# A third chunk's gelu by the activation table instead of the tanh formula, in a fused attention and gated feed-forward block

## The chip, the cores and the metric

One core of one Trainium2 chip. The metric is the device time of one execution in microseconds, the median of several runs. Lower is better.

## What is computed

A pre-norm block over 2048 tokens of width 640 in bf16: 32 heads of 20 for the attention, 1728 hidden columns for the gated feed-forward. There is no mask.

```python
def _A_ref(x, wqkv, wo):
    qkv = (x @ wqkv).reshape(B, S, 3, H, Dh).transpose(2, 0, 3, 1, 4)
    q, k, v = qkv[0], qkv[1], qkv[2]
    scores = jnp.einsum("bhqd,bhkd->bhqk", q, k) * (Dh ** -0.5)
    p = _softmax(scores, axis=-1)
    o = jnp.einsum("bhqk,bhkd->bhqd", p, v)
    return o.transpose(0, 2, 1, 3).reshape(B, S, D) @ wo
def _B_ref(x, w_gate, w_up, w_down):
    g = jnp.einsum("bsd,df->bsf", x, w_gate)
    u = jnp.einsum("bsd,df->bsf", x, w_up)
    return jnp.einsum("bsf,fd->bsd", jax.nn.gelu(g, approximate=True) * u, w_down)
x = A_x
h = x + _A_ref(_layernorm(x), A_wqkv, A_wo)
h2 = h + _B_ref(_layernorm(h), B_w_gate, B_w_up, B_w_down)
```

## The kernel before

The queries are cut into eight chunks (SIZES): 512, then five of 256, then two of 128 tokens. Counted from zero, chunks 0 to 7 start at tokens 0, 512, 768, 1024, 1280, 1536, 1792 and 1920. The third chunk of the title is chunk 2, tokens 768 to 1023. The heads come in eight groups of four. A slot is a chunk with as many groups as fill 512 columns, so there are 32 slots: eight for chunk 0, four for each chunk of 256, two for each of 128.

In a slot the scores of four heads are made in row groups of TensorE (L1081) in units of two or three PSUM banks. ScalarE takes the exponential of a unit of 1024 or 1536 columns (in the profile L450, `pts<-ps` and `rege<-ps`, which are two buffers). Part of the tiles go to VectorE instead (D_SLOT says how many), which makes an exponential from integer steps: one step out of PSUM (L992) and four terms (L450, TENSOR_SCALAR on 2048 columns); SUMS says how many pairs of terms are added first, and D_RING how many of these tiles take a bank of a ScalarE unit, which then shrinks from three tiles to two. The product with the values accumulates in bank 6 (L450, `ps<-pts,v_all` and the like). At a slot's end the sums are copied to `osb`, normalised and sent on; for the last slots of a chunk by transposes on TensorE (L1181), a reciprocal (L1187) and products (L1191).

When a chunk's attention is done, `post` makes the rest of the block for it, as background work beside the next chunk's attention: output projection (L758, L753 in its column form, L1274 in the last chunk), residual sum (L1285), layernorm, transposes, gate, gelu, up and down projection. The gate, up and down matmuls are L753 in the column form (four groups of 32 columns) and L1336, L1331 and L1405 otherwise; COL says from which chunk width on the column form is used and FULL which chunks do not use it. The gelu is made in one of two ways. Before TANH_FROM the gate is copied out of PSUM (L1379), and once all of it is out, the activation table's gelu runs over up to 2048 columns at a time. From TANH_FROM on, the gate is halved on the way out (L1373), and `gelu` makes three products and two scalar steps on VectorE and a tanh on ScalarE for pieces of up to 1024 columns. The up projection is multiplied in afterwards (L1390). The last chunk, which has no attention beside it, uses the gelu table (L1359, L1362), and its layernorm a root on ScalarE; its table loads are started early by one-column activations (`warmsq`, `warmge`).

The order on every engine is written out by a planner in the kernel (`Sched`). It goes through all operations with planned durations, priorities (P_...) and ages (QK_LEAD, PE_AGE, SD_AGE, SD_ROW: one value per slot), and emits for each engine one fixed queue with semaphore waits. An engine never passes a waiting instruction. The planner fills idle TensorE time with extra matmuls that change nothing. For ScalarE it knows modes, and a change of mode is planned with 1.28 us; a mode called "exp2", which only the formula's tanh has, is left out of that:

```python
op("act", I("activation", z, z, ACT.Tanh), c_act(w) + 0.04, -1, mode="exp2", reads=[zk], writes=[zk])
...
if o.mode is not None and o.mode != "exp2":
    if mode[e] not in (None, o.mode):
        o.dur += MODE_SWITCH[e]
    mode[e] = o.mode
```

The table loads themselves are put in when the program is compiled, wherever an activation needs another set than the one that is loaded.

At the start, maxima of the keys are taken (L792), combined (`kd`), and a bound for the scores is made from them (L891, L895); the first score waits for that. The first value projections (L907) are made beside it; `V_ACT` names those whose eviction ScalarE makes (L915) instead of VectorE (L917), `V_HOLD` from which set on they wait.

Of the kernel before, what the change touches and what calls it, by code (L numbers as in the profile page):

```python
# [18 lines left out]
DRAIN = {"pe": 0.165, "act": 0.118, "dve": 0.085, "pool": 0.05, "sp": 0.0}  # L19
WARM_WIN, WARM_MIN = 3.4, 0.5  # L20
PAD_WIN, PAD_MIN = 3.4, 0.42
QK_LEAD = (0.68, 0.72,) + (0.65,) * 4 + (0.72,) * 7 + (0.6,) * 4 + (0.72,) * 6 + (0.68, 0.68, 0.55, 0.55, 0.68, 0.65, 0.65, 0.68, 0.68,)
ACT_GAP = .012
PE_AGE = (2.5,) + (3.0,) * 5 + (5.0,) * 8 + (3.0,) * 3 + (5.0, 5.0, 2.0, 2.0,) + (5.0,) * 4 + (1.5, 1.5, 3.5, 3.0,) + (1.5,) * 3
SD_AGE = (0.6, 0.6, 0.3,) + (0.6,) * 6 + (0.8,) + (0.6,) * 5 + (1.0, 0.3, 0.6, 0.8, 0.6, 1.0, 0.5, 1.0, 1.0, 0.5,) + (0.6,) * 3 + (0.8,) * 4
SD_ROW = (0,) * 5 + (0.6,) * 4 + (1.5, 0.6, 0.6, 1.5,) + (0.6,) * 16 + (1.0, 0.6, 0,)
STOP = None


# [22 lines left out]
class Sched:  # L52
# [14 lines left out]
    def op(self, eng, fns, dur, prio, reads=(), writes=(), acq=(), rel=(), after=(), sem=None, lat=None, mode=None, util=0.0, rows=()):  # L67
        if eng == "dve" and rel and prio > self.ev:
            prio = self.ev
        o = Op()  # L70
        o.i = len(self.ops)
        o.eng, o.dur, o.lat, o.sem = eng, dur, DRAIN[eng] if lat is None else lat, sem
        o.util = util
        o.mode = mode
        o.rows = rows
        o.tag = writes[0] if writes else None
        o.fns = fns if isinstance(fns, list) else [fns]
        o.prio = (prio, o.i)
        deps = set(after)
        for r in reads:  # L80
            if r in self.lw:
                deps.add(self.lw[r])
        for w in writes:
            if w in self.lw:
                deps.add(self.lw[w])
            deps.update(self.rd.get(w, ()))
        for r in reads:
            self.rd.setdefault(r, []).append(o.i)
        for w in writes:
            self.lw[w] = o.i  # L90
            self.rd[w] = []
        deps.discard(o.i)
        o.deps = deps
        o.acq = list(acq)
        o.rel = list(rel)
        o.succ = []
        o.ready = 0.0
        self.ops.append(o)
        return o.i

    def schedule(self):
# [29 lines left out]
        while done < total:  # L131
# [6 lines left out]
            for e in ENGINES:  # L138
# [8 lines left out]
                while ready[e]:  # L147
# [18 lines left out]
                    if got and o.mode == "row" and 0 < p[0] < 1 and scores > 1 and t - o.ready < (  # L166
                            at(SD_AGE) if mode[e] != "row" else at(SD_ROW) if row_end[o.rows[0]] > max([row_start + 0.01] + [freed[b] for b in got]) + 0.02 else 0):
                        skipped.append((p, i))
# [89 lines left out]
                if e == "act":  # L258
                    act_end = max(act_end, t) + o.dur + ACT_GAP
                    o.fin = act_end + o.lat  # L260
                    due = act_end + (0.917 if o.dur > 1.2 else 1.344) - at(QK_LEAD) if o.mode == "exp" else None
                heapq.heappush(events, free[e])
# [104 lines left out]
PV_QUADS = 2  # L367
PR, PR2 = 13, 6
D_SLOT = (1,) + (3,) * 26 + (2, 3, 3, 0, 0,)
SUMS = (0,) + (1,) * 4 + (2, 2, 0, 0, 1, 0,) + (1,) * 3 + (0, 1, 1, 2, 3, 1, 0, 1, 1, 0, 2, 2, 1, 0, 1, 0, 3, 0,)  # L370
HOP = 3.2
D_LAT = 0.3
RECIP_MAGIC = float(0x7EF311C3)
# [6 lines left out]
RESV = 0.0  # L380
QK_LAT = 0.165
VN = 4
D_RING = (9,) * 4 + (6, 6,) + (9,) * 6 + (6,) * 16 + (12,) + (6,) * 3
D_FIRST = 0
D_SPAN = (16,) + (18,) * 13 + (17,) + (18,) * 4 + (19,) * 4 + (18,) * 7 + (17, 17,)
D0 = 8
P33 = ()
TANH_FROM = 768
GELU_A = 2.0 * 0.7978845608028654
GELU_B = 4.0 * GELU_A * 0.044715  # L390

P_EV = 1.8
P_QK, P_PV, P_TAIL, P_PRO, P_EPI, P_LN, P_BG = 0, 1, 1.2, 1.5, 2, 2.5, 3
P_KQ = (2, 3, 3, 3)
P_V1 = 3.0
P_V0 = 2.5
P_ON = 2.1
V_ACT = (0,)
XN_DVE = (7, 10, 13, 15)
VP = (0, 2, 5, 8)  # L400
V1 = ((0, 0, 0, 0, 0, 0, 0, 0, 1, 1, 1, 1, 1, 1, 1, 1), (2, 2, 2, 2, 3, 3, 3, 3, 3, 3, 3, 3, 4, 4, 4, 4))
X_LAT = 3.0
O_LAT = 3.2
HOP_L = 3.2
XP_PE = (6,)
HOLD = 3
P_KP = 1.6
K1_AFTER = 3
Q1_HOLD = 1
V_HOLD = 3  # L410
XD = ()
P_NOW = 1.05
P_K0 = 1.0
VB = (6, 7, 5)
K1_ACT = ()
FULL = (5,)
GROUPS = ((0, 4), (4, 7), (11, 5))
AG = (11, 5)
P_RS = 1.45
XORD = (0, 3, 1, 2)  # L420
P_DV = 0.5
P_ADD = 1.8
P_ST = 1.9
P_OUT = 2.5
LN_DVE = (0, 1, 2, 3, 4, 5, 6)
LATE = (0, 1, 2, 3, 4)

# [1 line left out]
def bass_sequential_preLN__mha_block__glu_gated_geglu__prompt_kernel(  # L429
# [12 lines left out]
    with ExitStack() as es:  # L442
# [492 lines left out]
        for s_, (c, gs) in enumerate(slots):  # L935
            mine = list(dict.fromkeys(x[1:3] for x in tiles if x[0] == s_))
            n = D_SLOT[s_]
            d_kb[s_] = [mine[(2 * i + 1) * len(mine) // (2 * n)] for i in range(n)]
            k = min(SUMS[s_], 2 * n)
            d_sums[s_] = [(i + 1) * k // max(n, 1) - i * k // max(n, 1) for i in range(n)]  # L940
# [5 lines left out]
        while rem:  # L946
# [8 lines left out]
            n = len(bs)  # L955
            ring.append(k[1] < want and n == 3 and (k[1] + 1) * D_RING[s_] // max(nd, 1) > k[1] * D_RING[s_] // max(nd, 1))
            n -= ring[-1]
# [170 lines left out]
        def spread(s, c, gs, nq):  # L1128
# [13 lines left out]
            for j in range(4):  # L1142
                h(bsum[32 * j:32 * j + 32, :], rdr[s, j].partition_broadcast(32), [("rdr", s)], ("bs", j), "sd", 0.36)
            op("dve", I("tensor_tensor", on16[:], osb[:, s, :], bsum[:], ALU.mult), c_dve(512), P_ON,
               reads=[("osb", s)] + [("bs", j) for j in range(4)], writes=["on16"])
# [4 lines left out]
        def epilogue(s_, bk):  # L1150
# [46 lines left out]
            if tail or not last:  # L1197
# [8 lines left out]
            op("sp", I("dma_start", oT[:, 0:na, tok], src[0:128 * na, :].rearrange("(a p) s -> p a s", p=128)), 0.4, P_EPI,  # L1206
               reads=ars, writes=hk, sem=f"oT{c}", lat=O_LAT + nq * 0.004, after=tuple(e_ops) if c == 0 else ())
            op("sp", I("dma_start", oT[0:pf, na, tok], src[128 * na:f0, :]), 0.4, P_EPI,
               reads=ars, writes=hk, sem=f"oT{c}", lat=O_LAT + nq * 0.004, after=tuple(e_ops) if c == 0 else ())
            todo = [(a, 0) for a in range(na + 1, NA)] + [(na, pf)]  # L1210
# [41 lines left out]
        def post(c, banks, tail):  # L1252
            p = P_TAIL if tail else P_LN
            q0, nq = CHUNKS[c]
            nt = nq // 128
            cl = nq >= COL and c not in FULL
            tb = base(c)
            hb = 1792 * tb
            first = tuple(e_ops) + tuple(last_qk[0]) + tuple(d_ops) if c == 0 else ()
            for tt in range(tb, tb + nt):  # L1260
# [5 lines left out]
                for hf in range(2):  # L1266
                    bk = Bank(*banks, after=LATE)
                    key = ("bk", sc_id())
                    if tail:
# [3 lines left out]
                        for a in range(NA):  # L1273
# [9 lines left out]
                    list(chain(bk, key, 320, [(oT[:, a, tt * 128:(tt + 1) * 128], wo[:, a, hf * 320:(hf + 1) * 320])  # L1283
                                              for a in range(NA)], [("hnT", tt), "wo"], p if tail else P_OUT, after=(sc.lw[("h", tt, hf)],), col=cl))
                    op("dve", lambda eng, bk=bk, tt=tt, hf=hf, i=i: eng.tensor_tensor(  # L1285
                        h_sb[:, tt, hf * 320:(hf + 1) * 320], bank(bk, 320), h_sb[:, tt, hf * 320:(hf + 1) * 320], ALU.add),
                       c_dve(320), p if tail else P_ADD, reads=[key, ("h", tt, hf)], writes=[("h", tt, hf)], rel=[bk], after=first)
                if tail:
# [76 lines left out]
            else:  # L1365

                cp, gl = [], []
                for k in range(nb):
                    bg, kg = mms(k, wg, "wg", tuple(x for key in hkeys(k) for x in sc.rd.get(key, ())))
                    w = cols(k)  # L1370
                    fv = hv(k, w)
                    if q0 >= TANH_FROM:
                        op("dve", lambda eng, bg=bg, fv=fv, w=w: eng.tensor_scalar(fv, bank(bg, w), 0.5, None, ALU.mult),  # L1373
                           c_dve(w), p, reads=[kg], writes=hkeys(k), rel=[bg])
                        if k % 2 or k == nb - 1:
# [4 lines left out]
                                 reads=[kg], writes=hkeys(k), rel=[bg], after=first))  # L1380
                for ks in [] if q0 >= TANH_FROM else [list(range(i, min(i + 4, nb))) for i in range(0, nb, 4)]:
                    w = 512 * (ks[-1] - ks[0]) + cols(ks[-1])
# [57 lines left out]
        for kts in v_sets(0):  # L1440
            proj_v(kts, 0, VB, P_EPI if kts[0] < VN else P_V0, "act" if kts[0] in V_ACT else "dve",
                   (sc.lw[HELD],) if HOLD and kts[0] >= V_HOLD else ())
        
        ui = 0
        for s_, (c, gs) in enumerate(slots):
# [37 lines left out]
            if gs[-1] == NG - 1:  # L1483
                tail = c == len(CHUNKS) - 1
                sc.ev = P_EV
                if c == 0:
# [36 lines left out]
```

## Time and profile before

| | |
|---|---|
| median of 3 runs | 866.83 us (866.38 to 867.52) |
| the profiled execution | 867.75 us, span 866.0 us |
| TensorE busy | 838.5 us (97%) |
| ScalarE busy | 838.4 us (97%), 8 table loads |
| VectorE busy | 750.4 us (87%) |
| granted TensorE clock | 0.998 |
| HBM traffic | 44 GB/s over the span |

In the rows of groups, `out<-in` are tiles by the program's names, then partitions x elements, the count, the busy time, the mean nanoseconds of one and the idle time of the engine ahead of it with its releaser. In the rows of the timeline, the first number is the start in microseconds, the second the length from the first start to the last end of a run of like instructions. The length of an instruction has a small overlap with the next one of its engine, so the distance from start to start is what it costs the queue. `regw`, `rege` and `qt_all` are large buffers that hold other things at other times: the gate of the feed-forward is in `rege`, the formula's intermediate in `qt_all`.

### The profile page before, as it was taken

The numbers are of one execution on the slowest core, as the hardware profiler recorded it, in microseconds if no ns is written. First come the engines' busy times: TensorE is split into PE (matmuls) and PEld (weight loads), VectorE is DVE, ScalarE is ACT, GpSimd is POOL, SyncE is SP. The second block draws the span as 40 slices with busy tenths as digits, with TensorE's granted clock in tenths as the row PEclk, the third lists the DMA queues.
The fourth block names the chain that finished last, engine by engine and source line by source line (L and its number), as shares of the span: only waits on it lengthen the run. The fifth ranks groups of instructions, "written<-read, shape, count | busy, mean of one in ns | idle before, by whom it ended". The sixth has DMA issues, their size and how long they took to land.

```text
span 866.0 us, 35545 instructions
## 1 busy us (share of the span) xinstructions
PE 838.5 (97%) x16215; PEld 420.4 (49%) x16215; DVE 750.4 (87%) x1372; ACT 838.4 (97%) x806; POOL 89.6 (10%) x268
## 2 busy tenths in 40 slices
PE   7999999999999899999999999999999999999998
PEld 5532332322343344445455555555554556666667
DVE  8769999999999799797899989999999897988344
ACT  7999999999999999999999999999999999999992
POOL 5001111110001110101002000011102110010000
PEclk9999999999999999999999999999999999999999
DMA  7212021223202642001110102010101101030000
GB/s 274 81 47 61 29 76 47 59 61 92 58 16 60 160 147 80 16 18 36 53 42 16 36 8 61 5 35 17 49 19 24 58 12 27 20 47 11 2 18 17
DMA packets 50173, 43.19 MB, mean 50 GB/s; under 512 B 21316, under 2 KB 44640, under 8 KB 50024
## 3 DMA queue, kind: packets, MB, share of 16 engines
q1 hardware_dynamic: 50024, 40.93, 16.8%
q8 instruction: 127, 2.08, 1.0%
q14 instruction: 22, 0.18, 0.1%
HBM read 27.95 MB, written 10.26 MB: 44 GB/s over the span
## 4 chain that ended last, share of the span: by engine, by line
ACT 51%; PE 39%; DVE 8%; issue 1%
ACT pts L450 35%; ACT rege L450 15%; PE ps L1081 11%; PE ps L450 10%; PE ps L753 9%; PE ps L758 3%; DVE qt_all L450 2%; DVE rege L450 2%; PE ps L907 1%; PE ps L1336 1%; DVE rege L992 1%; DVE qt_all L992 1%; PE ps L1405 1%; ACT qt_all L450 1%; PE ps L675 1%
## 5 line engine op out<-in xcount | busy, mean ns | idle before, releaser
L450 ACT ACTIVATE pts<-ps 128x1024 bf16<-128x1024 f32 (+1 forms) x496 | 558.5, 1240 | 2.8 <-PE ps L1081 2.2
L1081 PE MATMUL ps<-qt_all,kt_all 32*128 32x256 bf16 (+2 forms) x4096 | 304.0, 273 | 11.5 <-ACT pts L450 5.6
L450 ACT ACTIVATE rege<-ps 128x1024 bf16<-128x1024 f32 (+1 forms) x222 | 248.3, 1199 | 0.7 <-PE ps L1081 0.3
L1081 PEld LDWEIGHTS ps<-qt_all,kt_all 32*128 32x128 bf16 x4096 | 103.2, 92 | 202.8 <-ACT pts L450 90.6
L992 DVE TENSOR_SCALAR rege<-ps 128x512 int16<-128x512 f32 x220 | 148.5, 684 | 20.0 <-PE ps L1081 18.6
L450 PE MATMUL ps<-rege,v_all 128*21 128x256 bf16 (+2 forms) x2197 | 139.3, 286 | 0.5 <-DVE rege L450 0.5
L450 PE MATMUL ps<-pts,v_all 128*21 128x256 bf16 (+2 forms) x2403 | 124.8, 273 | 1.0 <-DVE osb L450 0.8
L753 PE MATMUL ps<-rege,regw 128*32 128x256 bf16 (+1 forms) x2600 | 120.5, 296 | 1.6 <-DVE rege L992 0.5
L992 DVE TENSOR_SCALAR qt_all<-ps 128x512 int16<-128x512 f32 x128 | 86.7, 683 | 11.0 <-PE ps L1081 10.2
L450 DVE TENSOR_SCALAR rege<-rege 128x2048 int16<-128x2048 int16 x141 | 94.5, 687 | 1.5 <-PE ps L450 0.8
L753 PEld LDWEIGHTS ps<-rege,regw 128*32 128x32 bf16 x2600 | 60.4, 96 | 34.6 <-issue 20.1
L450 PEld LDWEIGHTS ps<-rege,v_all 128*21 128x21 bf16 x2197 | 54.4, 91 | 41.6 <-issue 26.1
L450 PEld LDWEIGHTS ps<-pts,v_all 128*21 128x21 bf16 x2403 | 56.6, 91 | 26.0 <-issue 19.2
L450 DVE TENSOR_SCALAR qt_all<-qt_all 128x2048 int16<-128x2048 int16 (+4 forms) x113 | 65.4, 589 | 3.0 <-ACT qt_all L450 1.0
L753 PE MATMUL ps<-regw,rege 128*32 128x320 bf16 x1296 | 67.4, 301 | 0.3 <-DVE rege L992 0.3
L758 PE MATMUL ps<-regw 128*128 128x512 bf16 (+2 forms) x215 | 59.6, 368 | 0.4
L450 PE MATMUL ps<-qt_all,v_all 128*21 128x256 bf16 (+1 forms) x1264 | 56.5, 264 | 0.8 <-DVE qt_all L450 0.8
L450 DVE TENSOR_SCALAR qt_all<-rege 128x2048 int16<-128x2048 int16 x80 | 53.8, 684 | 1.6 <-PE ps L450 1.2
L450 POOL TENSOR_SCALAR rn<-rc 128x16 int32<-128x16 int32 x22 | 7.0, 317 | 461.7 <-DMA rc<-sums 461.6
L1390 DVE TENSOR_TENSOR rege<-rege,ps 128x512 bf16<-128x512 bf16 (+2 forms) x53 | 35.0, 661 | 13.0 <-PE ps L753 6.6
L1336 PE MATMUL ps<-rege,regw 128*128 128x128 bf16 (+1 forms) x420 | 40.9, 238 | 0.0
L753 PEld LDWEIGHTS ps<-regw,rege 128*32 128x32 bf16 x1296 | 30.0, 96 | 18.3 <-issue 10.8
(139 smaller groups left out, 805.7 us busy)
## 6 DMA issues: line engine op xcount, KB each, us to landing
bsum<-rsums SPq DMA_DIRECT2D x88, 64.0 KB, 2.1
rege<-in_A_x_dram SPq DMA_DIRECT2D x5, 640.0 KB, 5.8
q_rows<-regw SPq DMA_DIRECT2D x20, 128.0 KB, 1.8
out_dram<-rege SPq DMA_DIRECT2D x15, 160.0 KB, 1.8
regw<-in_B_w_gate_dram SPq DMA_DIRECT2D x5, 432.0 KB, 3.3
regw<-in_B_w_up_dram SPq DMA_DIRECT2D x5, 432.0 KB, 3.5
kt_all<-k_rows SPq DMA_DIRECT2D x12, 160.0 KB
qt_all<-q_rows SPq DMA_DIRECT2D x12, 160.0 KB
```

Source lines behind the costliest of these rows:

```text
L450: return lambda eng: getattr(eng, method)(*args, **kwargs)
L675: op("pe", lambda eng, a=a: eng.transpose(bank16(bk, D)[:, 128 * a:128 * a + 128], src[:, a * 128:(a + 1) * 128], ident[:]), 0.055, prio, ...
L753: return [lambda eng, j=j: eng.matmul(out()[32 * j:32 * j + 32], l[:, 32 * j:32 * j + 32], r, start=start, stop=stop, tile_position=(0, 32 ...
L758: fn = col4(lambda: bank(bk, n), l, r, k == 0, k == len(steps) - 1) if col else lambda eng, l=l, r=r, k=k: eng.matmul(bank(bk, n), l, r, s ...
L907: w_readers.append(op("pe", lambda eng, i=i, kt=kt, a=a: eng.matmul(bank(bk)[:, i * w:i * w + w], xnT[:, a, kt * 128:(kt + 1) * 128], wv[: ...
L992: d_ops.append(op("dve", lambda eng: eng.tensor_scalar(v[:, 512 * h:512 * h + 512], bank(b), EXP_MUL, -32000.0, ALU.mult, ALU.max), c_dve( ...
L1081: return lambda eng: eng.matmul(out()[:, kk * nq:(kk + 1) * nq], kt_all[32 * j:32 * j + 32, g, kt * 128:(kt + 1) * 128], qt_all[32 * j:32 ...
L1336: lambda eng, a=a, f=f, fi=fi: eng.matmul(bank(bk)[:, fi * nq:(fi + 1) * nq], w[:, a, F0[f]:F0[f] + 128], hnT[:, a, 128 * tb:128 * tb + nq ...
L1390: hdone.append(op("dve", lambda eng, bu=bu, fv=fv, w=w: eng.tensor_tensor(fv, fv, bank(bu, w), ALU.mult), c_dve(w), p, reads=[ku] + hkeys( ...
L1405: f == NF - 1) if cl else lambda eng, f=f, o=o, bk=bk, w0=w0, w1=w1: eng.matmul(
```

## The change

TANH_FROM goes from 768 to 1024, so that chunk 2 takes the table's gelu as chunks 0 and 1 do; chunks 3 to 6 keep the formula. With it come other values for a number of the planner's settings: leads and ages of some slots, one more pair sum in slot 6, more tiles of ScalarE's units given to VectorE in the last slots, priorities of evictions, residual sums, output projections and normalisation, a planned DMA time, and the eviction of the first values by VectorE.

```diff
-QK_LEAD = (0.68, 0.72,) + (0.65,) * 4 + (0.72,) * 7 + (0.6,) * 4 + (0.72,) * 6 + (0.68, 0.68, 0.55, 0.55, 0.68, 0.65, 0.65, 0.68, 0.68,)
+QK_LEAD = (0.68, 0.72,) + (0.65,) * 4 + (0.72,) * 3 + (0.55, 0.55, 0.72, 0.65, 0.6, 0.55, 0.6, 0.6,) + (0.72,) * 6 + (0.68, 0.68, 0.55, 0.55, 0.68, 0.65, 0.65, 0.68, 0.68,)
-SD_ROW = (0,) * 5 + (0.6,) * 4 + (1.5, 0.6, 0.6, 1.5,) + (0.6,) * 16 + (1.0, 0.6, 0,)
+SD_ROW = (0,) * 5 + (0.6,) * 4 + (1.5, 0.6, 0.6, 1.5,) + (0.6,) * 16 + (1.0, 0.3, 0.3,)
-SUMS = (0,) + (1,) * 4 + (2, 2, 0, 0, 1, 0,) + (1,) * 3 + (0, 1, 1, 2, 3, 1, 0, 1, 1, 0, 2, 2, 1, 0, 1, 0, 3, 0,)
+SUMS = (0,) + (1,) * 4 + (2, 3, 0, 0, 1, 0,) + (1,) * 3 + (0, 1, 1, 2, 3, 1, 0, 1, 1, 0, 2, 2, 1, 0, 1, 0, 3, 0,)
-D_RING = (9,) * 4 + (6, 6,) + (9,) * 6 + (6,) * 16 + (12,) + (6,) * 3
+D_RING = (9,) * 4 + (6, 6,) + (9,) * 6 + (6,) * 16 + (12,) + (9,) * 3
-TANH_FROM = 768
+TANH_FROM = 1024
-P_EV = 1.8
+P_EV = 1.5
-P_ON = 2.1
-V_ACT = (0,)
+P_ON = 2.4
+V_ACT = ()
-O_LAT = 3.2
+O_LAT = 2.6
-V_HOLD = 3
+V_HOLD = 2
-FULL = (5,)
+FULL = (5, 6)
-P_ADD = 1.8
+P_ADD = 0.6
-P_OUT = 2.5
+P_OUT = 1.1
```

## The prediction

> **What bounds the kernel now.** I read the page's busy line first, then the windows that hold the attention part (first to last exponential), then the chain of waits by line in stretches, and last the timeline of the tail.
>
> ```profile
> PE 838.5 (97%) x16215; PEld 420.4 (49%) x16215; DVE 750.4 (87%) x1372; ACT 838.4 (97%) x806; POOL 89.6 (10%) x268
> 32.84:841.50 808.66, 789.83 (x15679) 381.93 (x15678) 710.98 (x1260) 805.26 (x746) 77.86 (x237) 1.00 0.17 45
> 525.00:590.00 65.00, 63.90 (x1640) 36.38 (x1640) 64.41 (x120) 64.98 (x62) 7.76 (x22) 1.00 0.10 27
> by line: PE ps L753 25.4%; PE ps L1081 21.2%; PE ps L450 17.8%; DVE qt_all L450 11.2%; DVE qt_all L992 5.0%; DVE rege L450 4.9%; DVE rege L992 3.9%; DVE rege L1373 2.9%; DVE rege L1390 1.5%; ACT pts L450 1.1%; issue 1.0%; DVE rege L1285 1.0
> ```
>
> The second row (length, then busy time of PE, PEld, DVE, ACT, POOL) says that ScalarE is idle for 808.66 - 805.26 = 3.4 us in all between the first and the last exponential. The exponentials follow each other almost without a gap, so whatever is added to ScalarE there moves the last exponential, unless it goes into those 3.4 us. The third row is the stretch in which the third chunk's gelu is made: TensorE, VectorE and ScalarE are all above 98%. The fourth is the chain of waits by line for 600 to 725 us: there it runs over TensorE and VectorE with hardly any ScalarE. So three engines are in balance, and relief for one of them helps only as far as the others allow; ScalarE allows 3.4 us.
>
> **The gelu itself.** The changed program's order has 12 table loads instead of 8. Two of the four stand around two gelu instructions of 2048 and 1408 columns, after the 472nd exponential. The second chunk, of the same width, already does this, and the third chunk's formula pieces are three tanh of 1024 columns and one of 384:
>
> ```profile
> 480.62 1.28 ACT L450 ACT_TABLE_LOAD   x1
> 481.91 3.18 ACT L450 ACTIVATE rege<-rege 128x2048 bf16<-128x2048 bf16 x2
> 485.11 1.28 ACT L450 ACT_TABLE_LOAD   x1
> 486.40 3.28 ACT L450 ACTIVATE pts<-ps 128x1536 bf16<-128x1536 f32 x3
> 525.10 1.05 ACT L450 ACTIVATE qt_all<-qt_all 128x1024 f16<-128x1024 f16 x1
> 526.04 1.44 ACT L450 ACTIVATE pts<-ps 128x1536 bf16<-128x1536 f32 x1
> 589.75 0.65 ACT L450 ACTIVATE qt_all<-qt_all 128x384 f16<-128x384 f16 x1
> 590.16 2.50 ACT L450 ACTIVATE pts<-ps 128x1024 bf16<-128x1024 f32 x2
> ```
>
> From the first load to the next exponential are 486.40 - 480.62 = 5.78 us. A tanh of 1024 takes 526.04 - 525.10 = 0.94 from start to next start, one of 384 takes 0.41; three and one are 3.23. ScalarE gets **+2.55 us**. The tanh stands between exponentials with no load row.
>
> The Trainium skill, "ScalarE: Activation LUTs", section "Table sets: the hidden batching unit", says that exp and tanh share a loadable set and that calls should be grouped by set; this speaks against the change, and the tanh row agrees. Its section "What ACT_TABLE_LOAD costs" puts a switch at 1283 ns and a drain of some 1380 ns, 2.66 us in all. The load rows agree with the 1.28, but the gelu starts 1.29 us after the load does, so no such drain shows behind it.
>
> VectorE loses what the formula costs:
>
> ```profile
> L450 DVE TENSOR_SCALAR qt_all<-qt_all 128x1024 f16<-128x1024 f16 x26 | 10.9, 421 | 0.8 <-ACT qt_all L450 0.7
> L450 DVE TENSOR_TENSOR qt_all<-rege 128x1024 f16<-128x1024 bf16 x13 | 8.8, 681 | 0.1
> L450 DVE TENSOR_SCALAR qt_all<-qt_all 128x384 f16<-128x384 f16 x6 | 1.5, 251 | 0.0
> L450 DVE TENSOR_TENSOR qt_all<-rege 128x384 f16<-128x384 bf16 x3 | 1.0, 349 | 0.0
> L450 DVE TENSOR_TENSOR qt_all<-qt_all 128x2048 bf16<-128x2048 bf16 x9 | 10.9, 1213 | 0.0
> ```
>
> A piece has three products and two scalar steps: 3 x 0.68 + 2 x 0.42 = 2.88 us for 1024 columns, 3 x 0.35 + 2 x 0.25 = 1.55 for 384; 3 x 2.88 + 1.55 = 10.2 us go. The eviction of the gate is a copy instead of a product with 0.5, the same size. SUMS in slot 6 adds one pair sum (1.2 us) and takes four value matmuls from TensorE. By the windows this relief meets a ScalarE with no room, so I price it at nothing on the path. If its cover goes, that is, if ScalarE's waits for scores come from VectorE and vanish, it is worth up to the 3.4 us.
>
> **The start.** With V_ACT empty, the first value eviction leaves ScalarE for VectorE. The order puts it between the last maximum of the keys and the one that combines them (kd), on the way to the first score:
>
> ```profile
> 25.49 0.62 ACT L915 ACTIVATE v_all<-ps 128x480 bf16<-128x480 f32 x1
> 29.73 0.74 DVE L792 TENSOR_REDUCE km<-ps 128x1 f32<-128x128 f32 x2
> 30.51 0.16 DVE L450 TENSOR_REDUCE kd<-km 128x1 f32<-128x5 f32 x1
> 32.33 0.66 DVE L917 CAST v_all<-ps 128x480 bf16<-128x480 f32 x1
> 32.40 0.60 PE L1081 MATMUL ps<-qt_all,kt_all 32*128 32x512 bf16 x5
> ```
>
> VectorE gets 0.6 us ahead of kd; ScalarE's transposed copies come some 0.45 earlier, which lets the last maxima begin about 0.3 earlier. Net **+0.3 us** (between -0.3 and +0.6). V_HOLD holds the same sets as before, and FULL adds a chunk whose width of 128 never had the column form: both do nothing. D_RING in slot 29 makes three more exponentials of 1024 columns and two fewer of 1536:
>
> ```profile
> L450 ACT ACTIVATE pts<-ps 128x1024 bf16<-128x1024 f32 x300 | 308.2, 1073 | 0.9 <-PE ps L1081 0.6
> L450 ACT ACTIVATE pts<-ps 128x1536 bf16<-128x1536 f32 x196 | 293.0, 1495 | 1.9 <-PE ps L1081 1.6
> ```
>
> 3 x 1.07 - 2 x 1.50 = 0.2, less overlap: **+0.1**. The other settings (leads, ages, priorities, O_LAT) only reorder. I price them at nothing inside the attention part, with both ends kept: all of ScalarE's idle time gone (-3.4), or twice as much (+3.4).
>
> **The tail.** Here the order changes most. The last chunk's layernorm and the second-to-last chunk's feed-forward interleave after the last exponential:
>
> ```profile
> 840.43 1.11 ACT L450 ACTIVATE pts<-ps 128x1024 bf16<-128x1024 f32 x1
> 841.49 0.84 ACT L450 ACTIVATE qt_all<-qt_all 128x768 f16<-128x768 f16 x1
> 842.35 1.28 ACT L450 ACT_TABLE_LOAD   x1
> 843.23 0.75 DVE L450 COPY osb<-ps 128x256 f32<-128x256 f32 x2
> 844.51 0.26 DVE L1187 RECIPROCAL rc<-ps 128x16 f32<-128x16 f32 x1
> 844.80 0.68 DVE L1191 TENSOR_TENSOR qt_all<-ps,rc 128x80 bf16<-128x80 f32 x4
> 845.46 0.49 ACT L700 ACTIVATE rege<-ps 128x384 bf16<-128x384 bf16 x1 [1.61 <-PE ps L694]
> 846.00 1.53 PE L1274 MATMUL ps<-wo,rege 128*128 128x320 bf16 x10
> 847.58 0.50 DVE L1278 BATCH_NORM_STATS2 stats<-ps 128x6 f32<-128x320 f32 x1 [0.18 <-PE ps L1274]
> 848.11 0.21 DVE L450 BATCH_NORM_AGGREGATE mv<-stats 128x2 f32<-128x12 f32 x1
> 848.75 0.21 ACT L450 ACTIVATE sd<-sd 128x1 bf16<-128x1 bf16 x1 [0.20 <-DVE sd L450]
> 847.37 2.61 PE L1405 MATMUL ps<-regw,rege 128*128 128x320 bf16 x18
> 849.18 0.64 DVE L450 TENSOR_SCALAR xn_t<-rege,mu,rs 128x384 bf16<-128x384 bf16 x2
> 849.82 0.44 PE L694 MATMUL ps<-ident,xn_t 128*128 128x128 bf16 x5
> 851.46 7.98 PE L1336 MATMUL ps<-rege,regw 128*128 128x128 bf16 x140
> ```
>
> Let E be the end of the last exponential, 841.54 before. One tanh of 1024 columns that stood ahead of the last three exponentials now stands behind E: **-0.94** on E. Behind E the order holds four loads instead of two, because the planner gives its tanh no table of its own: the sqrt set (warm-up), the exp set again for the 768 tanh, the sqrt set again, gelu. Walking the new order with these durations, from E:
> - The rest of the value matmuls ends near 0.6, the two osb copies at 1.3 (before 2.4). Then VectorE has 0.46 + 0.40 + 0.61 of the formula's pieces ahead of the reciprocal, and a product of 0.5 ahead of the four normalisations, which end at 4.3 (before 3.9).
> - ScalarE: tanh to 0.9, load, warm-up, load to 3.7, tanh 768 (its input is ready at 3.6) to 4.6, copy L700 to 5.1 (before 4.4). L1274 runs 5.1 to 6.7.
> - VectorE makes L703, an L1390 and two formula steps meanwhile; the statistics end at 7.5 (before 6.5), an L1390 product follows, and the variance is ready at 8.7.
> - ScalarE's copies end at 7.95, and the reload of sqrt holds it to 9.2; the root ends at 9.5 (before 7.4). The reciprocal, another L1390 and the normalised row follow to 10.7 (before 8.3).
> - TensorE has 39 gate and up matmuls (0.057 each by the last row) after L1274, to 8.85. Its next, L1405, waits for that last L1390 (10.1), and the transposes for the row. Only then come 26 of the 28 L1405 ((849.82 - 847.37) / 18 = 0.136 each): 3.5 us, to 14.4. Before, 18 of them covered the layernorm.
>
> So the final 140 matmuls start at E + 14.4 instead of 851.46 - 841.54 = 9.9: **+4.5 us**. From there both orders are the same. The bounds are +1.4, if only the 24 more gate and up matmuls left at E count, and +5.1, if the instructions do not overlap as in these rows.
>
> **The sum.** 2.55 - 0.94 + 0.1 + 0.3 + 4.5 = +6.5 us: the profiled execution's 867.75 (span 866.0 and 1.75 around it) would become 874.2. The median of the runs is 0.92 below that execution: 866.83 + 6.5 = **873.3 us**. About 0.2% (1.7 us) is what a measurement can tell from no change.
>
> **Rivals.**
> - ScalarE's waits vanish: with 10.2 us less on VectorE and earlier evictions, scores are never late. For it speaks the chain of 600 to 725 us; against it, that only 3.4 us can come. 873.3 - 3.4 = 869.9. Chance 0.17.
> - That and the cheap tail together (-3.1): 866.8, no change. Chance 0.06.
> - Faster: VectorE, not ScalarE, sets the pace from 525 to 725 us. Then its relief of 10.2 - 1.2 - 0.7 = 8.3 us comes off whole: 873.3 - 8.3 = 865.0. It decides only if ScalarE's exponentials can close up by over 8 us; 3.4 us of idle time says no, unless small gaps hide inside its rows. Chance 0.09.
> - Slower still: the pause of 5.8 us comes while VectorE is full, and scores come late behind it, doubling the idle time: 876.7. Chance 0.10.
> - Each switch costs as much again as its load before the next function starts: 1.28 more at three loads on the path (two of the third chunk, the sqrt reload of the tail), 877.1. The gap of 0.01 between a load's end (480.62 + 1.28) and the gelu's start (481.91) denies it. Chance 0.02. The Trainium skill's 2.66 us per switch, cited above, would make it 4.1 and the sum 877.4.
> - That the change doesn't do what it says is excluded by its order.
>
> **The numbers.** The forecast has 0.56. The range is 867.5 to 877.0; outside lie the faster case, most of the unchanged one and the upper end of the slow ones. Faster 0.09, same 0.06, slower 0.85.
>
> **What would show it.** In the changed profile: 12 loads of 1.28; the gelu pause near 5.8 us around 550 to 570 us; the last exponential ending near 843.5; TensorE idle over 1 us between L1336 x39 and L1405; the last run of 140 L1336 about 14 us behind the last exponential. I am wrong if the last exponential ends before 841, or if that distance stays near 10.

## The result, and the profile after

| | before | after |
|---|---|---|
| median of 4 runs each, us | 866.61 (866.00 to 867.52) | 880.63 (879.51 to 881.05) |
| ratio, 95% interval | 1 | 1.0156 (1.0144 to 1.0168) |
| profiled execution, us (span) | 867.75 (866.0) | 880.24 (878.5) |

The changed kernel is slower by 14 us. The direction was forecast; the forecast was 873.3 us, and 880.6 lies outside the range of 867.5 to 877.0.

The lines of after that answer to those of before: the busy line of the page; the windows from the first exponential to the end of the last, and around the third chunk's gelu (length, then busy time of PE, PEld, DVE, ACT and POOL, granted clock, DMA share, GB/s).

```profile
PE 838.1 (95%) x16178; PEld 423.8 (48%) x16215; DVE 740.9 (84%) x1354; ACT 844.2 (96%) x808; POOL 92.8 (11%) x268
32.93:850.00 817.07, 787.40 (x15631) 383.93 (x15663) 698.79 (x1235) 807.97 (x746) 81.09 (x237) 1.00 0.17 45
550.00:590.00 40.00, 38.34 (x944) 20.86 (x944) 33.32 (x62) 39.85 (x37) 4.66 (x12) 1.00 0.08 21
```

ScalarE's busy time between these two points grew by 807.97 - 805.26 = 2.7 us, about what the gelu adds. Its idle time grew from 3.4 to 817.07 - 807.97 = 9.1 us. In the 40 us that hold the gelu's pause (its two table loads, with the gelu between them) it is idle for 0.15 us only.

The timeline of after shows where the idle time lies, in these rows of ScalarE (the bracket is the wait before the row, and what ended it), and how the end runs.

```profile
303.20 1.02 ACT L450 ACTIVATE rege<-ps 128x1024 bf16<-128x1024 f32 x1 [1.69 <-PE ps L1081]
304.54 1.02 ACT L450 ACTIVATE rege<-ps 128x1024 bf16<-128x1024 f32 x1 [0.32 <-PE ps L1081]
306.06 4.62 ACT L450 ACTIVATE pts<-ps 128x1536 bf16<-128x1536 f32 x4 [0.50 <-PE ps L1081]
...
438.86 3.33 ACT L450 ACTIVATE pts<-ps 128x1536 bf16<-128x1536 f32 x3 [2.52 <-PE ps L450]
...
564.17 1.28 ACT L450 ACT_TABLE_LOAD   x1
565.46 3.18 ACT L450 ACTIVATE rege<-rege 128x2048 bf16<-128x2048 bf16 x2
568.66 1.28 ACT L450 ACT_TABLE_LOAD   x1
569.95 3.28 ACT L450 ACTIVATE pts<-ps 128x1536 bf16<-128x1536 f32 x3
...
848.37 1.62 ACT L450 ACTIVATE rege<-ps 128x1536 bf16<-128x1536 f32 x1
...
857.59 1.28 ACT L450 ACT_TABLE_LOAD   x1
858.89 0.20 ACT L450 ACTIVATE sd<-sd 128x1 bf16<-128x1 bf16 x1
```
```profile
859.66 0.45 PE L1405 MATMUL ps<-regw,rege 128*128 128x320 bf16 x2 [0.92 <-DVE rege L1390]
...
860.33 3.69 PE L1405 MATMUL ps<-regw,rege 128*128 128x320 bf16 x26
863.86 7.98 PE L1336 MATMUL ps<-rege,regw 128*128 128x128 bf16 x140
```

A hole is a stretch in which ScalarE waits between two exponentials. Two of them, 2.5 us near 303 (three waits: 1.69 + 0.32 + 0.50) and 2.5 us near 439, make most of the new idle time. Both lie over 120 us ahead of the gelu. The span splits so: the first exponential starts 0.1 us later (32.93 against 32.84); first exponential to the end of the last, E, takes 849.99 - 32.93 = 817.06 against 808.70 us (+8.4); from E to the last run of gate and up matmuls 863.86 - 849.99 = 13.9 against 9.9 us (+3.95); the rest 14.6 against 14.5. Below, the first of these lengths is "the attention part" and the second "the tail".

### The profile page after: what moved, and what is told of

The parts are those of the page before. It is cut to its first block, busy times and chain, and to the rows that moved or that the text cites. A ratio compares the mean times of both kernels' runs of the same rounds, so it can differ in the third digit from the quotient of the medians.

```text
span 878.5 us, 35496 instructions
## 1 busy us (share of the span) xinstructions
PE 838.1 (95%) x16178; PEld 423.8 (48%) x16215; DVE 740.9 (84%) x1354; ACT 844.2 (96%) x808; POOL 92.8 (11%) x268
## 4 chain that ended last, share of the span: by engine, by line
ACT 46%; PE 39%; DVE 12%; DMA 1%; issue 1%; SPq 0%; DVEq 0%
ACT pts L450 30%; ACT rege L450 14%; PE ps L1081 12%; PE ps L753 10%; PE ps L450 10%; DVE qt_all L450 3%; PE ps L758 2%; PE ps L1336 2%; DVE rege L992 2%; DVE rege L450 2%; DVE qt_all L992 2%; PE ps L907 1%; DMA regw<-in_B_w_gate_dram 1%; PE ps L1405 1%; ACT L450 1%
## 5 line engine op out<-in xcount | busy, mean ns | idle before, releaser
L1081 PE MATMUL ps<-qt_all,kt_all 32*128 32x256 bf16 (+2 forms) x4096 | 309.3, 273 | 14.7 <-ACT pts L450 5.7
L1081 PEld LDWEIGHTS ps<-qt_all,kt_all 32*128 32x128 bf16 x4096 | 106.2, 92 | 207.2 <-ACT pts L450 92.6
L992 DVE TENSOR_SCALAR rege<-ps 128x512 int16<-128x512 f32 x220 | 148.6, 683 | 21.5 <-PE ps L1081 20.2
L753 PE MATMUL ps<-rege,regw 128*32 128x256 bf16 (+1 forms) x2600 | 121.8, 296 | 2.2 <-ACT rege L450 0.6
L992 DVE TENSOR_SCALAR qt_all<-ps 128x512 int16<-128x512 f32 x128 | 86.8, 685 | 19.4 <-PE ps L1081 19.2
L753 PEld LDWEIGHTS ps<-rege,regw 128*32 128x32 bf16 x2600 | 60.3, 96 | 38.5 <-issue 23.1
L753 PE MATMUL ps<-regw,rege 128*32 128x320 bf16 x1296 | 66.1, 301 | 0.4 <-DVE rege L1410 0.3
L450 DVE TENSOR_SCALAR qt_all<-qt_all 128x2048 int16<-128x2048 int16 (+4 forms) x105 | 62.3, 603 | 2.3 <-ACT qt_all L450 1.0
L758 PE MATMUL ps<-regw 128*128 128x512 bf16 (+2 forms) x189 | 52.2, 366 | 2.7 <-issue 1.4
L753 PEld LDWEIGHTS ps<-regw,rege 128*32 128x32 bf16 x1296 | 30.0, 96 | 16.3 <-issue 9.7
L1336 PE MATMUL ps<-rege,regw 128*128 128x128 bf16 (+1 forms) x420 | 37.3, 238 | 0.2 <-DVE sd L450 0.2
```

What stands on the lines that cost most here:

```text
L450: return lambda eng: getattr(eng, method)(*args, **kwargs)
L753: return [lambda eng, j=j: eng.matmul(out()[32 * j:32 * j + 32], l[:, 32 * j:32 * j + 32], r, start=start, stop=stop, tile_position=(0, 32 ...
L758: fn = col4(lambda: bank(bk, n), l, r, k == 0, k == len(steps) - 1) if col else lambda eng, l=l, r=r, k=k: eng.matmul(bank(bk, n), l, r, s ...
L992: d_ops.append(op("dve", lambda eng: eng.tensor_scalar(v[:, 512 * h:512 * h + 512], bank(b), EXP_MUL, -32000.0, ALU.mult, ALU.max), c_dve( ...
L1081: return lambda eng: eng.matmul(out()[:, kk * nq:(kk + 1) * nq], kt_all[32 * j:32 * j + 32, g, kt * 128:(kt + 1) * 128], qt_all[32 * j:32 ...
L1336: lambda eng, a=a, f=f, fi=fi: eng.matmul(bank(bk)[:, fi * nq:(fi + 1) * nq], w[:, a, F0[f]:F0[f] + 128], hnT[:, a, 128 * tb:128 * tb + nq ...
```

## The experiments

Theories at the start: **A**, the new order costs most, by the holes and the tail, and the gelu little; **B**, the gelu's pause disturbs what follows. A1 and A2 are A with a named culprit: the priorities P_ADD and P_OUT, or SyncE's queue near 303 us. Theories that came later (G, S, C, T) are named in the expectations where they are first put to a run. All ratios are to the kernel before, timed on the same chip. What each kernel measured, in us:

| run | what it is | median | ratio (95%) | attention | tail |
|---|---|---|---|---|---|
| before | | 866.6 to 867.7 | 1 | 808.70 | 9.92 |
| after | | 880.63 | 1.0156 (1.0144 to 1.0168) | 817.06 | 13.87 |
| e1 | gelu alone, order planned anew | 881.51 | 1.0164 (1.0149 to 1.018) | 812.04 | 20.25 |
| e2 | settings alone | 881.16 | 1.0167 (1.015 to 1.0184) | 815.75 | 15.07 |
| e3 | after, P_ADD and P_OUT back | 881.14 | 1.0162 (1.0147 to 1.0177) | 817.70 | 13.87 |
| e4 | after, sums ahead of weights | 881.6 | 1.0166 (1.0151 to 1.0181) | 816.88 | 13.86 |
| e6 | before's order, two loads | 871.69 | 1.0045 (1.003 to 1.006) | 811.90 | 9.93 |
| e10 | before's order, gelu | 872.0 | 1.0049 (1.0034 to 1.0063) | 813.57 | 9.93 |
| e14 | e10, TensorE kept busy | 869.45 | 1.002 (1.0011 to 1.0029) | 810.18 | 9.93 |
| e7 | before, SUMS alone | 884.66 | 1.0196 (1.0181 to 1.0211) | 816.10 | 20.19 |
| e9 | after, SUMS, O_LAT, QK_LEAD back | 884.41 | 1.0188 (1.0164 to 1.0212) | 813.68 | 22.52 |
| e11 | after, SUMS back | 878.18 | 1.0127 (1.0113 to 1.014) | 814.63 | 15.13 |
| e13 | before, D_RING alone | 868.77 | 1.0017 (1.0008 to 1.0026) | 809.81 | 10.42 |
| e12 | before, V_ACT alone | 867.65 | 1.0003 (0.9994 to 1.0011) | 807.82 | 9.93 |
| e5 | after, tail with two loads | 879.81 | 1.0146 (1.0133 to 1.016) | 818.02 | 13.12 |
| e15 | after, TensorE kept busy at 300 | 879.99 | 1.0158 (1.0138 to 1.0179) | 817.35 | 13.87 |

### The two halves of the change (e1, e2)

```diff
 # e1, from before:
-TANH_FROM = 768
+TANH_FROM = 1024
 # e2, from after:
-TANH_FROM = 1024
+TANH_FROM = 768
```

> The kernel before with TANH_FROM = 1024 alone; the planner makes a new order from it. Theory A (the settings that came with the change cost most of the 14 us, by two holes in ScalarE's exponentials near 303 and 439 us and by the tail): 866.6 plus the 2.55 us of ScalarE worked out for the gelu, 869 us, with 2 us either way for the new order. Theory B (the gelu pause itself disturbs the stretches behind it): over 875 us.

> The changed kernel with TANH_FROM back at 768, all other settings as changed. Theory A: the loss stays but for the gelu's 2.55 us, about 877 to 878 us. Theory B: the loss goes with the gelu, 868 to 870 us.

Each half alone costs as much as the whole, so the costs do not add. e1 came out as dear as theory B said and e2 dearer than theory A said, so neither theory holds as it was put. The two lose the time in different places. e1 has no hole over 0.3 us near 303 or 439 us; its attention part grew by 3.3 us and its tail by 10.3. e2 has both holes (1.03 and 0.50 us near 303, 2.51 at 437.44), without the third chunk's gelu. In e1's tail 84 gate and up matmuls and 28 down-projections of the second-to-last chunk stand behind the last chunk's layernorm, where before had 10 down-projections left:

```profile
855.70 4.89 PE L1336 MATMUL ps<-rege,regw 128*128 128x128 bf16 x84 [0.91 <-ACT rege L700]
860.42 3.97 PE L1405 MATMUL ps<-regw,rege 128*128 128x320 bf16 x28
864.23 7.20 PE L1336 MATMUL ps<-rege,regw 128*128 128x128 bf16 x126
```

Where it fell behind shows in windows of 50 us with only the matmuls of line L753 (feed-forward and output projection of the earlier chunks), first of before, then of e1; the columns are the length, TensorE's busy time on them and their count:

```profile
533.00:583.00 50.00, 23.19 (x572) 1.00 0.09 22
583.00:633.00 50.00, 22.47 (x516) 1.00 0.11 33
633.00:683.00 50.00, 22.20 (x452) 1.00 0.11 24
```
```profile
533.00:583.00 50.00, 20.21 (x480) 1.00 0.10 25
583.00:633.00 50.00, 21.54 (x464) 1.00 0.10 31
633.00:683.00 50.00, 15.92 (x392) 1.00 0.11 20
```

In these 150 us e1 makes 1336 of these matmuls where before makes 1540. The 204 missing are some 9 us of work at before's 67.86 / 1540 = 0.044 us each; what is not done there has to be done later, and 8.5 us of feed-forward (the 84 and the 28) ends behind the last exponential. The third chunk's gelu is not needed for this: e7 below, which keeps the formula, makes 480, 456 and 376 in the same windows, 1312 in all, and has the same 84 and 28 in its tail.

### Two suspects for the holes (e3, e4)

```diff
 # e3, from after:
-P_ADD = 0.6
+P_ADD = 1.8
-P_OUT = 1.1
+P_OUT = 2.5
 # e4, from after, in SyncE's queue near 290 us:
+the second gate-weight load behind rsums, the third behind bsum
```

> The changed kernel with P_ADD and P_OUT back at 1.8 and 2.5. Theory A1 (the hole of 2.52 us near 439 us comes from output projections and residual sums that stand ahead of scores and value products): that hole goes, and with its neighbourhood 2.5 to 3.5 us: 877 to 878. Rival (any new order has holes of its own; the priority does not matter): within 1 us of 880.6, with a hole of over 2 us elsewhere.

> The changed kernel with one thing moved in SyncE's queue: the second and third loads of the gate's weights are issued behind the softmax sums' transfers (rsums, bsum) that stood behind them; the orders of all other engines are the same. Theory A2 (the hole near 303 us comes from bsum, which waits in SyncE's queue behind a weight load that waits for the one before it): bsum lands about 5 us earlier, VectorE's wait of 4.2 us and ScalarE's of 1.69, 0.32 and 0.50 go: 3 us less, 877.5 us. Rival (bsum is late because the weights fill the DMA engines, or scores are late there for another reason): unchanged, 880.6.

e3 has the holes of after (2.21, 0.47 and 0.50 near 304, 2.51 at 439.94): A1 falls. The orders explain it: with either value every engine has the same instructions in the same order, so e3 is the same program as after, and its 0.5 us are what a repeat moves. That holds for P_EV, P_ON, V_HOLD, FULL and SD_ROW too, so seven of the twelve settings changed beside TANH_FROM move nothing.

The first hole, in after. VectorE, TensorE and SyncE's queue:

```profile
301.07 0.69 DVE L450 TENSOR_TENSOR on<-osb,bsum 128x512 bf16<-128x512 f32 x1 [4.23 <-DMA bsum<-rsums]
301.68 0.69 DVE L992 TENSOR_SCALAR qt_all<-ps 128x512 int16<-128x512 f32 x1
```
```profile
302.42 0.40 PE L753 MATMUL ps<-kt_all 128*32 128x512 bf16 x4 [2.40 <-DVE qt_all L992]
302.75 0.39 PE L1081 MATMUL ps<-qt_all,kt_all 32*128 32x256 bf16 x6
...
303.89 0.62 PE L1081 MATMUL ps<-qt_all,kt_all 32*128 32x256 bf16 x6
```
```profile
296.01 0.33 SPq L450 DMA_DIRECT2D regw<-in_B_w_gate_dram  x1
296.39 1.82 SPq L450 DMA_DIRECT2D bsum<-rsums  x4
```

The sums that VectorE waits for are issued behind a weight load, which itself stands in the queue until 296.01. VectorE waits 4.23 us with the scores' eviction (L992) behind it, TensorE 2.40 us for that, ScalarE 1.69 us for scores. In e4, where the sums go first, VectorE waits 0.96 us instead of 4.23, but the weights land later: TensorE waits 1.82 us for them at 306.90, and ScalarE has holes of 1.65 at 308.53 and 1.12 at 310.67. The attention part stays at 816.9 us. So the place of the sums makes VectorE's wait, but swapping it with the weights only moves the hole; A2 alone doesn't explain the loss. The weights do come late: the last of the five gate loads is issued at 303.88 us in after, at 299.33 in before.

VectorE in before shows what else is new:

```profile
302.06 0.69 DVE L992 TENSOR_SCALAR qt_all<-ps 128x512 int16<-128x512 f32 x1 [0.42 <-PE ps L1081]
303.03 0.69 DVE L450 TENSOR_TENSOR on<-osb,bsum 128x512 bf16<-128x512 f32 x1 [0.28 <-DMA bsum<-rsums]
```

There the last of the sums is issued later still, at 299.72 us, and does no harm, because the product that reads them stands behind three evictions of scores (298.73, 300.95 and 302.06). In after it stands ahead of them, and holds them up. No run moves this product alone.

The second hole, in after, has no transfer in it:

```profile
436.34 0.60 PE L1081 MATMUL ps<-qt_all,kt_all 32*128 32x256 bf16 x6
...
438.41 0.39 PE L450 MATMUL ps<-pts,v_all 128*21 128x256 bf16 x8
```

ScalarE's wait ends at 438.86, just behind the value matmuls of 438.41, which read `pts`, the buffer that the waiting exponential writes. Between these two rows TensorE's queue has 32 matmuls of L753 and 16 other value matmuls, and no wait.

### One setting for both holes (e7, e9, e11)

```diff
 # e7, from before; e11 undoes this in after:
-SUMS = (0,) + (1,) * 4 + (2, 2, 0, 0, 1, 0,) + ...
+SUMS = (0,) + (1,) * 4 + (2, 3, 0, 0, 1, 0,) + ...
 # e9, from after: SUMS, QK_LEAD and O_LAT as in before
```

> The kernel before with one number changed, SUMS of slot 6 from 2 to 3 (one more pair sum, four value matmuls fewer); the gelu stays the formula. The new order differs from the 435th row of TensorE's on, and leaves 84 gate and up matmuls and 28 down-projections of the second-to-last chunk behind the last chunk's layernorm. Theory A: any new order costs: tail about 20 us instead of 10 as with the gelu alone, holes near 303 us, 877 to 882 us. Theory G (the gelu is what costs, by its pause or its relief): no gelu, no cost, 866 to 868 us.

> The kernel after with QK_LEAD, SUMS and O_LAT as before; of the settings that move an instruction only D_RING of the last slots and V_ACT stay, with the gelu. Theory A: the holes at 303 and 439 us come from the three settings and go; the last exponential ends about 2.5 to 3.5 us later than before, and the tail is that of the gelu alone (83 gate and up and 28 down-projections behind the layernorm, 20 us): 880 us. If the holes come from the gelu or from the first exponential's place, they stay, and 885 us.

> The kernel after with SUMS of slot 6 back at 2 and all else as changed, the gelu included. Theory S (the one pair sum of slot 6 makes the holes near 303 and 439 us): both go, from first to last exponential 812 to 814 us instead of 817.1, and the tail by its order (65 gate and up and 28 down-projections after the projection of the last chunk) is about 15 us: 876 to 878 us. If the gelu or another setting makes them, they stay and it is 881 us or more.

e7 has no gelu of the third chunk and one number changed. ScalarE's rows in it:

```profile
301.59 1.02 ACT L450 ACTIVATE rege<-ps 128x1024 bf16<-128x1024 f32 x1 [1.69 <-PE ps L1081]
302.95 1.02 ACT L450 ACTIVATE rege<-ps 128x1024 bf16<-128x1024 f32 x1 [0.33 <-PE ps L1081]
...
436.55 3.33 ACT L450 ACTIVATE pts<-ps 128x1536 bf16<-128x1536 f32 x3 [2.52 <-PE ps L450]
```

These are the holes of after, to a hundredth, but for the third wait near 303 (0.50 us), which e7 lacks. Its product with the sums waits 3.92 us ahead of the evictions, as in after. In e9 and e11, with SUMS back and the gelu kept, both holes are gone; e11 there, in ScalarE's timeline without one bracket:

```profile
299.52 3.09 ACT L450 ACTIVATE rege<-ps 128x1024 bf16<-128x1024 f32 x3
302.35 5.70 ACT L450 ACTIVATE pts<-ps 128x1536 bf16<-128x1536 f32 x5
...
438.03 5.14 ACT L450 ACTIVATE pts<-ps 128x1024 bf16<-128x1024 f32 x5
```

So one pair sum more in slot 6 makes both holes, the gelu neither: theory S holds, and G (no gelu, no cost) falls with e7's 884.66 us. What the holes are worth in after is less than their 5 us: e11's attention part is 2.4 us shorter, as it has new holes (1.14 us at 748 and 1.19 at 778), and its tail 1.3 longer; in time it gains 2.4 us (880.63 to 878.18).

e7 is dearer than theory A said, and e9 too: with QK_LEAD and O_LAT back beside SUMS the holes go, but the tail is 22.5 us where e11 has 15.1. So one or both of these two settings shorten the tail that the gelu's new order has.

### The gelu in the old order (e6, e10, e14)

```diff
 # e6, from before: ahead of one tanh of the third chunk
+gelu of one column (two table loads)
 # e10, from before: third chunk; the formula is left out
-tensor_tensor / tensor_scalar of the formula on 128x1024, 128x384
+the same on 128x1
-third tanh 128x1024
+Gelu_apprx_tanh 128x1024 (two table loads)
 # e14, from e10: on TensorE behind the pause
+48 matmuls 128x512 with a zero operand
```

> The kernel before, every engine's order as it was, and the formula kept; only a gelu of one column stands ahead of the third chunk's second tanh, which brings two table loads (2 x 1.28 us) in between two exponentials. Theory A (the pause itself is cheap, the new order is dear): ScalarE has 3.4 us of idle time in the whole attention part, so it gets 2.6 to 2.9 us longer, 869.7 us, ratio 1.003, and the distance from the last exponential to the last run of gate and up matmuls stays at 10 us. Theory B (the pause disturbs what follows): a hole of over 2 us behind it, 873 us or more. If TensorE's work sets the end and ScalarE's pause is covered: under 867.5.

> The kernel before, every engine's order as it was; for the third chunk the formula's five VectorE steps shrink to one column each (the formula is left out there), and its third tanh of 1024 columns becomes a gelu of the table with its two loads. So ScalarE gets 2.6 us and VectorE loses some 9 us, as in the change, without any new order. Theory A: 869.4 us, ratio 1.003, relief of VectorE worth nothing. Rival (VectorE sets the pace between 525 and 725 us): the relief shows whole or in part, 861 to 866 us. Theory B: 873 us or more.

> The kernel before with the same order and the third chunk's table gelu put in it (formula left out there), as in the earlier run with the same order, which took 4.3 us more than the kernel before; new are 48 matmuls with a zero operand (about 2.6 us) in the 2.67 us in which TensorE had nothing to do behind the two table loads. Theory C (the pause is dear because TensorE stands still in it and its granted clock then falls to 0.50 for some 7 us): the clock stays at 1.00 behind the pause, the hole of 1.13 us at 593 us goes, and the time is 1 to 2 us less, 870.5 us, ratio 1.0035. If the clock has nothing to do with it, the hole stays and the ratio is 1.005.

With every engine's order kept, the tail stays at 9.93 us in all three: no new order, no longer tail. VectorE's 6 us less (745.3 us busy in e10 against 751.3 in e6, by their pages) bring nothing that can be measured (872.0 against 871.69 us), so it does not set the pace there. But the pause costs 4 us, not the 2.6 us of its two loads: more than theory A said, less than B. TensorE and the windows of e10 show why (the granted clock, 1.00 when it is full, is the third number from the end):

```profile
584.50 0.95 PE L753 MATMUL ps<-rege,regw 128*32 128x256 bf16 x28 [0.52 <-DVE rege L992]
588.12 0.62 PE L1081 MATMUL ps<-qt_all,kt_all 32*128 32x256 bf16 x8 [2.67 <-ACT pts L450]
```
```profile
584.00:586.00 2.00, 0.95 (x28) 0.66 (x28) 2.00 (x4) 1.97 (x3) 0.96 (x3) 1.00 0.04 4
586.00:588.00 2.00, 0.00 (x0) 0.00 (x0) 0.27 (x1) 1.99 (x3) 1.50 (x7) 0.68 0.00 0
588.00:590.00 2.00, 1.88 (x32) 0.88 (x32) 1.18 (x2) 2.00 (x3) 0.33 (x2) 0.50 0.05 4
590.00:592.00 2.00, 2.00 (x36) 1.08 (x32) 0.90 (x3) 1.34 (x2) 0.00 (x0) 0.50 0.17 41
592.00:594.00 2.00, 2.00 (x38) 0.94 (x31) 0.86 (x4) 1.13 (x1) 0.00 (x0) 0.61 0.28 98
```

ScalarE's pause leaves TensorE without work for 2.67 us; then the granted clock is 0.50 until 593 us, and ScalarE runs out of scores (a hole of 1.13 us at 592.87). e14 fills the gap with matmuls that change nothing:

```profile
584.41 2.76 PE L452 MATMUL ps<-kt_all,zer 128*32 128x512 bf16 x48
```
```profile
586.00:588.00 2.00, 1.92 (x48) 0.87 (x44) 0.26 (x1) 1.99 (x3) 1.35 (x7) 1.00 0.00 0
588.00:590.00 2.00, 2.00 (x59) 1.13 (x55) 2.00 (x4) 2.00 (x3) 0.00 (x0) 1.00 0.05 4
```

The clock stays at 1.00, the hole is gone, and the gelu costs 869.45 - 867.4 = 2.05 us. The exponentials say the same: from the first to the 521st it is 581.78 us in before, 586.60 in e10 and 584.33 in e14, so 4.8 us later with the standstill and 2.5 without. Theory C holds: the clock is a cause. In after itself the pause of the gelu is free of this, as every window of 2 us from 560 to 580 us has a clock of 1.00.

### The clock behind the first hole (e15)

```diff
 # from after: at the value matmuls of 299.6 us
+44 matmuls 128x512 with a zero operand
```

> The kernel after with 44 matmuls with a zero operand (about 2.4 us) in the 2.40 us in which TensorE waits for VectorE before 302.4 us; nothing else changed. Theory C: the granted clock stays at 1.00 from 302 to 308 us, where it was 0.82, 0.50 and 0.83, the second and third hole of ScalarE there (0.32 and 0.50 us) go and the first (1.69 us, which the late weights and sums make) stays: 0.8 to 1.2 us less, 879.6 us, ratio 1.0147. If the clock is only a mark of the hole and not its cause, all three stay: 880.6 us, 1.0156.

The granted clock of after in windows of 2 us, and ScalarE's rows of e15 at that place:

```profile
300.00:302.00 2.00, 0.02 (x4) 0.00 (x0) 0.93 (x2) 1.50 (x2) 0.00 (x0) 1.00 0.54 161
302.00:304.00 2.00, 1.58 (x15) 0.45 (x18) 1.66 (x3) 0.80 (x1) 0.00 (x0) 0.82 0.31 107
304.00:306.00 2.00, 2.00 (x18) 0.34 (x19) 0.69 (x1) 1.24 (x2) 0.00 (x0) 0.50 0.47 104
306.00:308.00 2.00, 1.63 (x31) 0.70 (x29) 0.69 (x1) 1.94 (x2) 0.41 (x2) 0.83 0.35 125
```
```profile
302.26 1.94 ACT L451 ACTIVATE rege<-ps 128x1024 bf16<-128x1024 f32 x2 [1.58 <-PE ps L1082]
304.09 4.63 ACT L451 ACTIVATE pts<-ps 128x1536 bf16<-128x1536 f32 x4
```

In e15 the clock stays at 1.00, the second and third hole go and the first stays, as theory C said; exponential by exponential it is then 1.1 us ahead of after, up to 434 us. That lead is lost by 792 us, where the two timelines differ by 0.3 us the other way, with new holes of 0.71 and 0.81 us at 776 and 780 us. The attention part is 817.35 us long against 817.06, and the ratio cannot be told from that of after. The local mechanism is shown; a gain in time from it is not.

### Small parts (e12, e13, e5)

```diff
 # e12, from before:
-V_ACT = (0,)
+V_ACT = ()
 # e13, from before:
-D_RING = ... + (12,) + (6,) * 3
+D_RING = ... + (12,) + (9,) * 3
 # e5, from after: the 768-column piece of the second-to-last chunk
-ACT.Tanh
+ACT.Copy
```

> The kernel before with V_ACT empty and nothing else changed: only the start's order differs. The forecast put +0.3 us on it (-0.3 to +0.6): 867.3 us. Whether this part of the change is worth keeping alone: below 866.5 it would beat the kernel before.

> The kernel before with D_RING's last three slots at 9 and nothing else changed. By its order the last run of 140 gate and up matmuls has all 28 down-projections of the second-to-last chunk ahead of it as before, but 17 instead of 10 of them behind the last layernorm's transposes: +1.0 us in the tail, and +0.1 for the exponentials, 868 us. Theory A (any new order costs over 10 us) says 877 to 882 us; theory T (what counts is how much of the second-to-last chunk's feed-forward is left behind the last exponential, and here it is as much as before) says 868.

> The kernel after, every engine's order as it was, with the 768-column tanh of the second-to-last chunk's formula replaced by a copy (that part of the formula is wrong), so that the tail needs two table loads instead of four. If the reloads were on the path, as forecast: the root of the last layernorm no longer waits for the second load of its set, and the tail is 0.5 to 1.3 us shorter, 879.5 to 880.3 us. If they are covered by the matmuls of the feed-forward: 880.8 us, unchanged.

e12's time is no change that can be measured. e13 costs 1.3 us and not ten: not every new order is dear. Its tail has all 28 down-projections ahead of the last run, as before has, and grew by 0.5 us; "any new order costs" falls, and theory T (what counts is the feed-forward left behind the last exponential) holds here. e5's root stands at 858.77 with E at 850.92, 7.85 us behind E instead of 8.90, and the tail is 0.75 us shorter: the reloads were on the path, for that much.

No kernel run here beats the kernel before.

## Why the prediction was wrong

- **The failed step** is the one that priced the settings inside the attention part at nothing: SUMS was counted as one pair sum and four value matmuls less, worth nothing on the path, and the other settings "only reorder", with ends of -3.4 and +3.4 us. Attention grew by 8.4 us where the terms gave 2.55 - 0.94 + 0.1 = 1.7; 2.7 of the 8.4 are ScalarE's own work and 5.7 are idle time. SUMS alone opens both holes (e7, and their absence in e9 and e11). Undone in after it gives back 2.4 us of the attention part; the 3.1 us of idle time that e11 still has above before (814.63 - 808.15 = 6.48 against 3.4) belong to the rest of the new order, which no run takes apart. The bound was worked out from ScalarE's total idle time in a tuned order, and nothing makes the idle time of another order a multiple of that.
- **The gelu.** Twelve loads, at the forecast places, and a pause of 569.95 - 564.17 = 5.78 us as forecast; the window of 550 to 590 us shows next to no idle time around it. ScalarE's +2.55 us is 2.05 us in time when TensorE is kept at work (e14). The gelu starts 1.29 us after its load does, here too, so the rival of a switch that costs its load twice falls. The drain of some 1380 ns that the Trainium skill ("ScalarE: Activation LUTs", "What ACT_TABLE_LOAD costs") states does not show here either.
- **VectorE's relief at nothing** was right in the old order (e6 against e10), and so the faster rival with VectorE's pace fell.
- **The start**, +0.3: the two profiles give +0.1 (32.93 against 32.84), but the first exponential of one and the same start moves by up to 1.2 us from one execution to the next, later where the clock falls for a stretch between 10 and 20 us. In the profiles whose clock is 1.00 in that window it starts at 31.93 to 31.94 us with V_ACT as before (e1, e7, e14) and at 32.20 to 32.23 as changed (e2, e11, e12, e15), so the +0.3 was right.
- **D_RING**, +0.1: alone it cost 1.3 us (e13); in its profile the attention part is 1.1 us longer and the tail 0.5. Two executions of one order differ by as much as 0.9 us in the attention part (e12 against before), so the place is less sure than the time.
- **The tail**, +4.5: it measured +3.95. The chain went as walked: the reload holds the root to 858.89, TensorE waits at 859.66, 26 of 28 down-projections come behind the transposes of the normalised row, and the last run starts 13.9 us behind E (forecast 14.4).
- **The rivals.** "The pause doubles the idle time" (876.7 us) fell short by 3.9 us and had the wrong mechanism: idle time grew by 5.7 us, most of it at 303 and 439 us, not behind the pause. The range's upper end was the sum with that one bound, and so too low.

The sum redone with what was measured: 0.1 + 8.4 + 3.95 + 0.1 = 12.5 us of span, 866.0 to 878.5. The direction was forecast for reasons that held, the gelu's work and the tail, and the two together are about half of the loss. That holds for the whole change only: either half of it alone costs as much.

What stays open: why the planner, given one more pair sum in slot 6, near 200 us, orders VectorE and TensorE so 100 and 240 us later, and why it leaves the feed-forward over 200 matmuls behind from 533 to 683 us, with the gelu alone (e1) and with the pair sum alone (e7). The runs show both, not the planner's step that does it. O_LAT and QK_LEAD were not tried alone.

## What to carry to other kernels

Where a planner makes the order, read the new order against the old as part of the change, and price it by two things that the orders show: what each in-order queue puts ahead of the work that the next scores wait for (here a product that waits for a transfer, ahead of three evictions), and how many matmuls are left behind the last exponential. A setting that moves one instruction early can cost more than the change that it came with, so try each half of a change alone and the operation alone in the old order. And do not bound the cost of a reordering by the idle time of the order that it replaces.

## What the runs showed of the hardware

TensorE's granted clock fell to 0.50 around standstills of 2.67 us (e10), 2.58 us (e6, ahead of 548.86) and 2.40 us (after, ahead of 302.42), and also of 1.82 us (e4, ahead of 306.90) and 1.74 us (e2, ahead of 301.06). Around one of 1.37 us (e7, ahead of 857.16) it stayed at 1.00. In e10 the window of 586 to 588 us lacks 0.64 us of clock, 1.28 us at half, so the fall came near 586.7, some 1.3 us after the last matmul ended (584.50 + 0.95). In after a score group of six matmuls took 0.62 us at 303.89, at half clock, and 0.39 at 302.75. In after the three windows that are below 1.00 lack 0.36 + 1.00 + 0.34 = 1.7 us of clock, which is 3.4 us at half; in e10 four windows lack 0.64 + 1.00 + 1.00 + 0.78 = 3.4, which is 6.8 us at half. With the gap filled, it stayed at 1.00 (e14, e15). The Trainium skill, "TensorE: Matmul & The Clock Gate", Part 1 on the HAM clock gate, describes a free-running activity window of some 3.4 us, after an idle one of which the array runs at half clock until a busy one. The half clock and the lengths of 3.4 and twice 3.4 us agree; that a whole window must be idle does not, as 1.3 us without a matmul went ahead of the fall in e10.
